# Earlier inputs in the load queues, and scores of a head pair on the two row halves of TensorE

## The chip, the cores and the metric

The kernel runs on one core of a Trainium2 chip. The metric is the device time of one execution in microseconds; several runs are taken and their median is given. One further execution is profiled: each instruction has its start, its length and what released it. A span is the time from the first to the last instruction of that execution.

The engines are TensorE (PE in the profile, its weight loads are PEld), VectorE (DVE), ScalarE (ACT), GpSimd (POOL) and SyncE (SP). Here SyncE does nothing but issue the loads of inputs and the stores; GpSimd issues the loads of weights beside its own work.

## The reference

Linear attention with a decay per head, in blocks, and behind it a layer norm with a two-layer MLP and a residual:

```
B, H, S, D = 4, 8, 768, 64                       # q, k, v in float32
for each block of the sequence:
    intra = ((q k^T) * Dmask) v                  # Dmask[i, j] = lam**(i-j) for i >= j, else 0
    inter = (q * lam**(i+1)) state
    out   = intra + inter
    state = lam**block * state + (k * lam**(block-1-i))^T v
x   = out as (B, S, H*D)                         # 512 wide
xn  = (x - mean) / sqrt(var + 1e-6) * g_ln
out = x + relu(xn @ w_ch1) @ w_ch2               # 512 -> 2048 -> 512
```

## The kernel before, in words

The 3072 rows (4 batches of 768) are cut into 24 tiles of 128 rows, six in a batch. Each tile passes five steps, and the heads go in four pairs, since two heads of 64 fill 128 partitions:

- `p0`/`bf_inputs` (lines 139 to 147, 289 to 292): GpSimd casts k to bf16 (`kb`), and multiplies q and v by powers of lam into bf16 (`qb`, `vb`). For tiles 4 and later `p0` also orders the load of tile t + 4.
- `p1` (149 to 168): PE transposes k and q, four transposes each. ScalarE copies k's transpose out of PSUM in two halves: head 0 of each pair to partitions 0 to 63 of one slot, head 1 to partitions 64 to 127 of another slot of `kTp`. The rest of `kTp` was set to zero once (lines 112 to 116), so that a matmul over all 128 partitions gives the score of one head alone.
- `p2` (170 to 196): the pair's k^T v (`pk`), from which VectorE and GpSimd make the next state (`Stmp`, `Sn`); eight score matmuls (line 192), four heads into each of two PSUM tiles `sc`; VectorE multiplies each by the mask into `mA`.
- `p3` (198 to 217): eight output matmuls on `mA` and `vb` (line 203), four on the state (207); ScalarE copies the result to `x`, VectorE makes mean and variance and the centred `xc`.
- `p4` (219 to 236): PE transposes `xc`, ScalarE copies it to `xT` of the tile's group and takes the root for the norm.

The MLP works on groups of tiles (`sizes`, line 284): `m1` (line 254) is layer 1 with ScalarE's relu behind it, `m2` (line 267) layer 2 of one tile in four parts of four matmuls, each part reading one of the four w2 chunks.

The order of the work is written out by hand (manual schedule; each engine works through its instructions in program order). Lines 309 to 354 place the first eight tiles and groups 0 to 3 one by one; `units` and `after` say which attention steps stand behind which MLP unit. From line 356 on a planner spreads the remaining attention steps (`round_of`: `p1`, `p3_p0`, `p2`, `p4`) evenly over the MLP units of groups 4 to 9, so that all steps of a group's tiles stand before its first `m1`.

Loads go through two queues. Inputs are issued by SyncE (k, q, v of a tile, 256 KB each, line 65), with six buffers each. Weights are issued by GpSimd (four chunks of w1, four of w2, lines 75 and 78), in its program order between casts. `load_tile(4, after_pool=True)` has GpSimd write one column of the buffer first, so SyncE's load waits until GpSimd has come that far. The steps concerned:

```python
run((p1, 0), (p2, 0), (p0, 2), (p1, 1), (p3, 0), (p2, 1))
load_w1(0); load_w1(1)
...
load_w1(3)
load_tile(4, after_pool=True)
for c in range(NWC): load_w2(c)
...
p0(4)            # casts of tile 4, behind three quarters of group 0's layer 1
```

Of the kernel before, what the change touches and what calls it, by code (L numbers as in the profile page):

```python
# [7 lines left out]
F32 = mybir.dt.float32  # L8
BF16 = mybir.dt.bfloat16
I32 = mybir.dt.int32  # L10
ALU = mybir.AluOpType
# [5 lines left out]
def kernel(  # L17
# [11 lines left out]
    nc = tc.nc  # L29
    B, H, S, D = q.shape  # L30
    C = 128
    nb = S // C
    NT = B * nb
    DM = H * D
    DF = moe_w_ch1.shape[1]
    NP = H // 2
# [9 lines left out]
    const = ctx.enter_context(tc.tile_pool(name="const", bufs=1))  # L46
    inp = ctx.enter_context(tc.tile_pool(name="inp", bufs=6))
    wk = ctx.enter_context(tc.tile_pool(name="wk", bufs=3))
    xp = ctx.enter_context(tc.tile_pool(name="xp", bufs=11))
    gp = ctx.enter_context(tc.tile_pool(name="gp", bufs=2))  # L50
    ps = ctx.enter_context(tc.tile_pool(name="ps", bufs=1, space=PSUM))


    qkv_in = {}

    def load_tile(t, after_pool=False):
        b, c = divmod(t, nb)
        got = {}
        for name, src in (("k", k), ("q", q), ("v", v)):
            f = inp.tile([128, H, D], F32, tag=name + "in", name=name + "in")  # L60
            if after_pool:

                nc.gpsimd.memset(f[:, 0, 0:1], 0.0)
                after_pool = False
            nc.sync.dma_start(f, src[b, :, c * C:(c + 1) * C, :].rearrange("h p d -> p h d"))
            got[name] = f
        qkv_in[t] = got
# [6 lines left out]
    def load_w1(c):  # L74
        nc.gpsimd.dma_start(w1[c], moe_w_ch1[:, c * W1C:(c + 1) * W1C].rearrange("(k p) f -> p k f", p=128))
# [20 lines left out]
    tril = const.tile([128, 128], F32)  # L96
# [12 lines left out]
    nc.vector.memset(eps_t, eps)  # L109
    lamC = const.tile([128, NP, 128], F32)  # L110
    nc.vector.memset(lamC, 0.0)
    kTp = []
    for i in range(2):
        kt = const.tile([128, NP, 2, 128], BF16, name=f"kTp{i}")
        nc.vector.memset(kt, 0.0)
        kTp.append(kt)

    lnlam = const.tile([128, H], F32)
    nc.scalar.activation(lnlam, lam_b, ACT.Ln)
# [4 lines left out]
    lam_c = const.tile([128, H], F32)  # L124
    nc.scalar.activation(lam_c, lnlam, ACT.Exp, scale=float(C))
    sqrt_first = const.tile([128, 1], F32)
    nc.scalar.activation(sqrt_first, eps_t, ACT.Sqrt)
    lam_cp = lam_c.rearrange("p (a two) -> p a two", two=2)
    nc.vector.tensor_copy(lamC[0:64, :, 0:64], lam_cp[0:64, :, 0:1].to_broadcast([64, NP, 64]))
    nc.vector.tensor_copy(lamC[64:128, :, 64:128], lam_cp[64:128, :, 1:2].to_broadcast([64, NP, 64]))  # L130


    st = {}
# [2 lines left out]
    mv_keep = {}  # L136
    xT_of = {}

    def bf_inputs(t):
        f = qkv_in.pop(t)  # L140
        kb = wk.tile([128, H, D], BF16, tag="kb", bufs=4, name="kb")
        nc.gpsimd.tensor_copy(kb, f["k"])  # L142
        qb = wk.tile([128, H, D], BF16, tag="qb", name="qb")
        nc.gpsimd.tensor_tensor(qb, f["q"], lam_q[:, :, None].to_broadcast([128, H, D]), op=ALU.mult)  # L144
        vb = wk.tile([128, H, D], BF16, tag="vb", bufs=4, name="vb")
        nc.gpsimd.tensor_tensor(vb, f["v"], lam_v[:, :, None].to_broadcast([128, H, D]), op=ALU.mult)  # L146
        st[t] = dict(qb=qb, kb=kb, vb=vb)

    def p1(t):
        s = st[t]  # L150
        tk = ps.tile([128, NP, 128], BF16, tag="aux", bufs=2, name="tk")
        for p in range(NP):
            nc.tensor.transpose(tk[:, p, :], s["kb"][:, 2 * p:2 * p + 2, :], ident)  # L153
        kT = kTp[t % 2]
        nc.scalar.copy(kT[0:64, :, 0, :], tk[0:64, :, :])  # L155
        nc.scalar.copy(kT[64:128, :, 1, :], tk[64:128, :, :])  # L156
        if t < 4:
            tq = ps.tile([128, NP, 128], BF16, tag="mm", bufs=3, name="tq")
        else:
            tq = ps.tile([128, NP, 128], BF16, tag="aux", bufs=2, name="tq")  # L160
        for p in range(NP):
            nc.tensor.transpose(tq[:, p, :], s["qb"][:, 2 * p:2 * p + 2, :], ident)  # L162
        qT = wk.tile([128, NP, 128], BF16, tag="qT", name="qT")
        if t < 4:
            nc.scalar.copy(qT, tq)
        else:
            nc.vector.tensor_copy(qT, tq)  # L167
        s["kT"], s["qT"] = kT, qT

    def p2(t):  # L170
        s = st[t]
        c = t % nb
        s["S"] = state.get("S") if c > 0 else None
        if c < nb - 1:
            pk = ps.tile([128, NP, 128], F32, tag="aux", bufs=2, name="pk")
            for p in range(NP):
                nc.tensor.matmul(pk[:, p, :], lhsT=s["kb"][:, 2 * p:2 * p + 2, :], rhs=s["vb"][:, 2 * p:2 * p + 2, :],  # L177
                                 start=(p == 0), stop=(p == NP - 1), skip_group_check=True)
            Sn = wk.tile([128, NP, 128], BF16, tag="S", name="Sn")
            if c == 0:  # L180
                nc.vector.tensor_tensor(Sn, pk, lamC, op=ALU.mult)
            else:
                tmp = wk.tile([128, NP, 128], F32, tag="Stmp", bufs=2, name="Stmp")
                nc.vector.tensor_tensor(tmp, pk, state["S"], op=ALU.add)  # L184
                nc.gpsimd.tensor_tensor(Sn, tmp, lamC, op=ALU.mult)  # L185
            state["S"] = Sn
        mA = wk.tile([128, H, 128], BF16, tag="mA", name="mA")
        for half in range(2):
            sc = ps.tile([128, H // 2, 128], F32, tag="sc", bufs=2, name="sc")
            for i in range(H // 2):  # L190
                h = half * (H // 2) + i
                nc.tensor.matmul(sc[:, i, :], lhsT=s["kT"][:, h // 2, h % 2, :], rhs=s["qT"][:, h // 2, :],  # L192
                                 start=(i == 0), stop=(i == H // 2 - 1), skip_group_check=True)
            nc.vector.tensor_tensor(mA[:, half * (H // 2):(half + 1) * (H // 2), :], sc,  # L194
                                    tril[:, None, :].to_broadcast([128, H // 2, 128]), op=ALU.mult)
        s["mA"] = mA

    def p3(t):
        s = st[t]
        po = ps.tile([128, H, D], F32, tag="po", bufs=1, name="po")  # L200
        inter = s["S"] is not None
        for h in range(H):
            nc.tensor.matmul(po[:, h, :], lhsT=s["mA"][:, h, :], rhs=s["vb"][:, h, :],  # L203
                             start=(h == 0), stop=(not inter and h == H - 1), skip_group_check=True)
        if inter:
            for p in range(NP):
                nc.tensor.matmul(po[:, 2 * p:2 * p + 2, :], lhsT=s["qT"][:, p, :], rhs=s["S"][:, p, :],  # L207
                                 start=False, stop=(p == NP - 1), skip_group_check=True)
        x = xp.tile([128, DM], F32, tag="x", name="x")
        nc.scalar.copy(x, po.rearrange("p h d -> p (h d)"))  # L210
        stats = wk.tile([128, 6], F32, tag="stats", name="stats")
        nc.vector.bn_stats(stats, x)  # L212
        mv = xp.tile([128, 2], F32, tag="mv", name="mv")
        nc.vector.bn_aggr(mv, stats)
        xc = wk.tile([128, DM], BF16, tag="xc", name="xc")
        nc.vector.scalar_tensor_tensor(xc, in0=x, scalar=mv[:, 0:1], in1=g_row, op0=ALU.subtract, op1=ALU.mult)  # L216
        s["xc"], s["mv"], s["x"] = xc, mv, x
# [63 lines left out]

        return m1, m2

    sizes = [2, 2, 1, 1, 2, 3, 3, 4, 4, 2]
    groups = [list(range(sum(sizes[:i]), sum(sizes[:i + 1]))) for i in range(len(sizes))]
    assert groups[-1][-1] == NT - 1
    group_of = {t: g for g, ts in enumerate(groups) for t in ts}

    def p0(t):
        if t > 3 and t + 4 < NT:  # L290
            load_tile(t + 4)
        bf_inputs(t)


    def p3_p0(t):
        p3(t)
        if t + 3 < NT:
            p0(t + 3)

    def round_of(j):  # L300
        steps = [(p1, j), (p3_p0, j - 1), (p2, j), (p4, j - 2)]
        return [(f, t) for f, t in steps if t < NT]

    def run(*steps):
        for f, *a in steps:
            f(*a)


    p0(0)
    p0(1)  # L310
    run((p1, 0), (p2, 0), (p0, 2), (p1, 1), (p3, 0), (p2, 1))
    load_w1(0)
    load_w1(1)
    run((p1, 2), (p3, 1))
    p0(3)
    load_w1(2)
    run((p2, 2), (p4, 0), (p1, 3), (p3, 2), (p2, 3), (p4, 1))
    load_w1(3)
    load_tile(4, after_pool=True)
    for c in range(NWC):  # L320
        load_w2(c)
    load_tile(5, after_pool=True)
# [5 lines left out]
    def m1s(f, c):  # L328
        for u in range(c * m1a.count // NWC, (c + 1) * m1a.count // NWC):
            f(u)  # L330
# [3 lines left out]
    m1s(m1a, 1)  # L334
    p4(3)
    m1s(m1a, 2)
    p0(4)
    for c in range(3):
        m1s(m1b, c)
    m1s(m1a, 3)  # L340
# [14 lines left out]

    steps = []
    for j in range(8, NT + 2):
        steps += [s for s in round_of(j) if s not in ((p3_p0, 7), (p4, 7), (p4, 6))]

    def upto(g):  # L360
        return steps.index((p4, groups[g][-1])) + 1 if g < len(groups) else len(steps)
# [47 lines left out]
```

## Time and profile before

| | us |
|---|---|
| median of 3 runs (lowest to highest) | 247.38 (247.32 to 247.84) |
| the profiled execution | 246.76 |
| its span | 245.0 |
| PE busy in it | 219.0 (89%) |
| ACT / DVE / POOL busy | 121.1 / 112.9 / 92.9 |

Busy shares are means over a start in which inputs arrive one by one, a stretch in which weights and inputs are loaded together, and a long stretch of matmuls. PE's granted clock has two levels here, 1.2 and 2.4 GHz; the view by stage gives their mean as a share of 2.4. The ends of matmuls are modelled, so starts are the surer numbers: in the chain of waits a group of matmuls runs to the start of the next, in the timeline to the modelled end of its last.

### The profile page before, as it was taken

Reading aid. Unit: us, or ns where it says so; the run is one execution under the profiler, and the core shown is the slowest. Engines: PE = TensorE matmul, PEld = TensorE weight load, DVE = VectorE, ACT = ScalarE, POOL = GpSimd, SP = SyncE. Lnnn points to the kernel's source line nnn. Section 1 sums busy time; section 2 is a strip of 40 time slices with the busy share of each in tenths; the row PEclk is TensorE's granted clock in tenths of the full one; section 3 lists DMA queues with packets and bytes.
Section 4 is the critical chain, followed back from the end, with each engine's and each line's share of the span. In section 5 each row is a group of like instructions: output and inputs, shape, how many; then the busy total and the mean of one; then the engine's idle time right before and its main releaser. Section 6 shows DMA issues by size and latency. Waiting matters only on the chain.

```text
span 245.0 us, 4603 instructions
## 1 busy us (share of the span) xinstructions
PE 219.0 (89%) x1856; PEld 142.2 (58%) x1856; DVE 112.9 (46%) x217; ACT 121.1 (49%) x236; POOL 92.9 (38%) x107
## 2 busy tenths in 40 slices
PE   0676894499999897999999999999999999999993
PEld 0565683354587586767755676555555544444851
DVE  3366700033547656798547655475346531122111
ACT  5745775002175366657863487427862247611520
POOL 2779710159500866791566293063322000000000
PEclk9999999689999999999999999999999999999999
DMA  6999999999899999329951960111001120012102
GB/s 127 236 195 146 147 188 196 218 210 210 188 300 208 235 229 219 67 63 237 221 84 43 225 120 4 43 47 43 0 3 43 43 86 3 0 43 88 43 0 86
DMA packets 83012, 29.91 MB, mean 122 GB/s; under 512 B 75568, under 2 KB 79920, under 8 KB 82992
## 3 DMA queue, kind: packets, MB, share of 16 engines
q1 hardware_dynamic: 78624, 25.43, 48.0%
q0 software_dynamic: 4224, 4.19, 10.7%
q8 instruction: 14, 0.23, 0.4%
q14 instruction: 6, 0.05, 0.1%
q10 hardware_dynamic: 144, 0.00, 0.0%
HBM read 27.53 MB, written 6.29 MB: 138 GB/s over the span
## 4 chain that ended last, share of the span: by engine, by line
PE 76%; DMA 8%; ACT 6%; DVE 5%; POOL 2%; issue 2%; DVEq 0%; SPq 0%; ACTq 0%
PE pm L267 33%; PE pm L254 28%; DMA qin<-in_q_dram 7%; PE sc L192 4%; PE po L203 2%; PE xt L230 2%; PE tk L153 2%; PE tq L162 2%; PE po L207 2%; PE pk L177 1%; DVE stats L212 1%; DMA lam_b<-in_lam_dram 1%; ACT kTp L155 1%; ACT x L210 1%; ACT kTp L156 1%
## 5 line engine op out<-in xcount | busy, mean ns | idle before, releaser
L254 PE MATMUL pm<-xT,w 128*128 128x256 bf16 (+3 forms) x640 | 92.6, 298 | 0.7 <-ACT xT L231 0.7
L267 PE MATMUL pm<-w,hT 128*128 128x512 bf16 x384 | 90.5, 381 | 0.0
L257 ACT ACTIVATE hT<-pm 128x512 bf16<-128x512 f32 (+1 forms) x104 | 58.1, 564 | 41.2 <-PE pm L254 40.6
L254 PEld LDWEIGHTS <-w 128*128 128x128 bf16 x640 | 56.9, 99 | 23.8 <-issue 0.8
L267 PEld LDWEIGHTS <-hT 128*128 128x128 bf16 x384 | 36.1, 98 | 36.1 <-issue 0.6
L185 POOL TENSOR_TENSOR Sn<-Stmp,lamC 128x512 bf16<-128x512 f32 x16 | 20.4, 1273 | 69.0 <-DVE Stmp L184 69.0
L212 DVE BATCH_NORM_STATS2 stats<-x 128x6 f32<-128x512 f32 x24 | 16.7, 695 | 46.2 <-ACT x L210 46.1
L278 DVE SCALAR_TENSOR_TENSOR o<-pm,rstd,x 128x512 f32<-128x512 f32 (+1 forms) x25 | 18.0, 725 | 32.7 <-PE pm L267 32.5
L231 ACT COPY xT<-xt 128x512 bf16<-128x512 bf16 x24 | 14.0, 584 | 37.1 <-PE xt L230 37.0
L194 DVE TENSOR_TENSOR mA<-sc,tril 128x512 bf16<-128x512 f32 x48 | 30.7, 680 | 0.0
L144 POOL TENSOR_TENSOR qb<-qin,lam_q 128x512 bf16<-128x512 f32 x24 | 25.8, 1074 | 12.1 <-DMA qin<-in_q_dram 8.6
L146 POOL TENSOR_TENSOR vb<-vin,lam_v 128x512 bf16<-128x512 f32 x24 | 25.5, 1060 | 3.4 <-DMA vin<-in_v_dram 3.0
L155 ACT COPY kTp<-tk 64x512 bf16<-64x512 bf16 x24 | 13.7, 572 | 16.9 <-PE tk L153 16.8
L210 ACT COPY x<-po 128x512 f32<-128x512 f32 x24 | 14.1, 586 | 14.7 <-PE po L207 11.0
L142 POOL CAST kb<-kin 128x512 bf16<-128x512 f32 x24 | 16.6, 690 | 10.8 <-DMA kin<-in_k_dram 10.7
L216 DVE SCALAR_TENSOR_TENSOR xc<-x,mv,g_row 128x512 bf16<-128x512 f32 x24 | 20.2, 840 | 0.9
L162 PE MATMUL tq<-ident,qb 128*128 128x128 bf16 x96 | 10.4, 237 | 11.1 <-POOL qb L144 9.5
L167 DVE COPY qT<-tq 128x512 bf16<-128x512 bf16 x20 | 8.4, 419 | 21.5 <-PE tq L162 21.5
L153 PE MATMUL tk<-ident,kb 128*128 128x128 bf16 x96 | 10.2, 234 | 7.6 <-POOL kb L142 7.6
L192 PE MATMUL sc<-qT,kTp 128*128 128x128 bf16 x192 | 16.4, 234 | 0.3 <-ACT kTp L156 0.2
L192 PEld LDWEIGHTS <-kTp 128*128 128x128 bf16 x192 | 13.5, 106 | 1.3 <-ACT kTp L156 0.4
L156 ACT COPY kTp<-tk 64x512 bf16<-64x512 bf16 x24 | 13.9, 580 | 0.6
(43 smaller groups left out, 127.0 us busy)
## 6 DMA issues: line engine op xcount, KB each, us to landing
kin<-in_k_dram SPq DMA_DIRECT2D x24, 256.0 KB, 4.8
qin<-in_q_dram SPq DMA_DIRECT2D x24, 256.0 KB, 5.1
vin<-in_v_dram SPq DMA_DIRECT2D x24, 256.0 KB, 5.1
out_dram<-o SPq DMA_DIRECT2D x23, 256.0 KB, 2.2
w<-in_moe_w_ch_dram POOLq DMA_DIRECT2D x8, 512.0 KB, 8.7
g_row<-in_moe_g_ln_dram SPq DMA_DIRECT2D x1, 256.0 KB, 4.8
out_dram<-o SPq DMA_DIRECT2D x2, 128.0 KB, 1.7
lam_b<-in_lam_dram ACTq DMA_DIRECT2D x1, 4.0 KB, 3.0
```

Source lines behind the costliest of these rows:

```text
L142: nc.gpsimd.tensor_copy(kb, f["k"])
L144: nc.gpsimd.tensor_tensor(qb, f["q"], lam_q[:, :, None].to_broadcast([128, H, D]), op=ALU.mult)
L146: nc.gpsimd.tensor_tensor(vb, f["v"], lam_v[:, :, None].to_broadcast([128, H, D]), op=ALU.mult)
L185: nc.gpsimd.tensor_tensor(Sn, tmp, lamC, op=ALU.mult)
L192: nc.tensor.matmul(sc[:, i, :], lhsT=s["kT"][:, h // 2, h % 2, :], rhs=s["qT"][:, h // 2, :], start=(i == 0), stop=(i == H // 2 - 1), skip ...
L194: nc.vector.tensor_tensor(mA[:, half * (H // 2):(half + 1) * (H // 2), :], sc, tril[:, None, :].to_broadcast([128, H // 2, 128]), op=ALU.mult)
L212: nc.vector.bn_stats(stats, x)
L216: nc.vector.scalar_tensor_tensor(xc, in0=x, scalar=mv[:, 0:1], in1=g_row, op0=ALU.subtract, op1=ALU.mult)
L254: nc.tensor.matmul(pm[:, b, :], lhsT=w1[n // W2K][:, kk, (n % W2K) * 128:(n % W2K + 1) * 128], rhs=xT_of[g][:, kk, 0:N], start=(b == 0 and ...
L257: nc.scalar.activation(hT[:, u * NB:(u + 1) * NB, 0:N], pm, ACT.Relu)
L267: nc.tensor.matmul(acc[i], lhsT=hT[:, kk, i * 128:(i + 1) * 128], rhs=w2[kk // W2K][:, kk % W2K, :], start=(kk == 0), stop=(kk == KB - 1))
L278: nc.vector.scalar_tensor_tensor(o[:, sl], in0=a[:, sl], scalar=rstd, in1=x[:, sl], op0=ALU.mult, op1=ALU.add)
```

## The change

- k is cast by VectorE for tiles 0 and 1 and by ScalarE for tiles 2 and 3; GpSimd casts k from tile 4 on, and q and v as before.
- The loads of w1 chunks and of tile 4 move: chunk 0 behind tile 2's casts, chunk 1 and then tile 4's inputs behind tile 3's, chunks 2 and 3 behind the next steps. `p0(4)` (GpSimd's casts of tile 4) moves ahead of the issues of w2. Tiles 5 to 7 are loaded behind w2, as before; tiles 8 and 9 are ordered together in `p0(5)`.
- k's transposes are kept compact: one copy of 128 partitions per tile into `kT`, no zeros. A score matmul takes the 64 partitions of its head, so the two heads of a pair use the upper and the lower row half of PE, one after the other in program order, each into its own PSUM tile. `mA` is laid out by even and odd heads.
- `sizes` becomes [2, 2, 1, 1, 2, 2, 3, 4, 4, 3], and in the planner `p4` comes one round earlier up to tile 10.

```diff
+    def in_k(t, eng):
+        kb = wk.tile([128, H, D], BF16, tag="kb", bufs=4, name="kb")
+        (eng.copy if eng is nc.scalar else eng.tensor_copy)(kb, qkv_in[t]["k"])
+        st[t] = dict(kb=kb)
+
+    def in_qv(t):
         f = qkv_in.pop(t)
-        kb = wk.tile([128, H, D], BF16, tag="kb", bufs=4, name="kb")
-        nc.gpsimd.tensor_copy(kb, f["k"])
...
-        kT = kTp[t % 2]
-        nc.scalar.copy(kT[0:64, :, 0, :], tk[0:64, :, :])
-        nc.scalar.copy(kT[64:128, :, 1, :], tk[64:128, :, :])
+        kT = wk.tile([128, NP, 128], BF16, tag="kT", name="kT")
+        nc.scalar.copy(kT, tk)
...
+        mA = wk.tile([128, 2, NP, 128], BF16, tag="mA", name="mA")
+        sc = [ps.tile([128, NP, 128], F32, tag="sc", bufs=2, name=f"sc{e}") for e in range(2)]
+        for p in range(NP):
+            for e in range(2):
+                half = slice(e * D, (e + 1) * D)
+                nc.tensor.matmul(sc[e][:, p, :], lhsT=s["kT"][half, p, :], rhs=s["qT"][half, p, :],
+                                 start=(p == 0), stop=(p == NP - 1), skip_group_check=True)
+        for e in range(2):
+            nc.vector.tensor_tensor(mA[:, e], sc[e], tril[:, None, :].to_broadcast([128, NP, 128]), op=ALU.mult)
...
-            nc.tensor.matmul(po[:, h, :], lhsT=s["mA"][:, h, :], rhs=s["vb"][:, h, :],
+            nc.tensor.matmul(po[:, h, :], lhsT=s["mA"][:, h % 2, h // 2, :], rhs=s["vb"][:, h, :],
...
-    sizes = [2, 2, 1, 1, 2, 3, 3, 4, 4, 2]
+    sizes = [2, 2, 1, 1, 2, 2, 3, 4, 4, 3]
...
-        if t > 3 and t + 4 < NT:
-            load_tile(t + 4)
-        bf_inputs(t)
+        for n in {4: (), 5: (8, 9)}.get(t, (t + 4,)):
+            if n < NT:
+                load_tile(n)
+        in_k(t, nc.gpsimd)
+        in_qv(t)
...
-        steps = [(p1, j), (p3_p0, j - 1), (p2, j), (p4, j - 2)]
+        steps = [(p1, j), (p3_p0, j - 1), (p2, j)]
+        if j <= 11:
+            steps.append((p4, j - 1))
+        elif j > 12:
+            steps.append((p4, j - 2))
...
+    run((p1, 0), (p2, 0), (p1, 1), (p3, 0))
+    in_k(2, nc.scalar)
+    in_qv(2)
     load_w1(0)
+    run((p2, 1), (p1, 2), (p3, 1))
+    in_k(3, nc.scalar)
+    in_qv(3)
     load_w1(1)
...
+    load_tile(4, after_pool=True)
+    run((p2, 2), (p4, 0), (p1, 3), (p3, 2))
     load_w1(2)
...
     load_w1(3)
-    load_tile(4, after_pool=True)
+    run((p2, 3), (p4, 1), (p0, 4))
     for c in range(NWC):
         load_w2(c)
     load_tile(5, after_pool=True)
...
     m1s(m1a, 2)
-    p0(4)
```

## Rows read from the trace of the kernel before

**Rows 1.** Work by stage: stretch, engines' busy us (instructions), granted clock, DMA share, GB/s.
```profile
40.00:46.60 6.60, 0.64 (x6) 0.58 (x7) 0.00 (x0) 1.02 (x2) 1.04 (x1) 0.84 1.21 196
46.60:60.00 13.40, 13.40 (x82) 7.47 (x81) 4.10 (x8) 2.56 (x5) 8.36 (x9) 0.82 1.09 215
75.00:100.00 25.00, 21.81 (x283) 18.34 (x282) 15.89 (x30) 14.33 (x27) 14.51 (x15) 1.00 1.09 222
150.00:175.00 25.00, 25.00 (x196) 14.18 (x195) 14.01 (x27) 13.42 (x28) 8.50 (x9) 1.00 0.09 32
```

**Rows 2.** The chain of waits in order of time: start us, us, what.
```profile
28.69 16.11 DMA qin<-in_q_dram
...
49.99 1.59 PE pm L267 x4
...
52.25 2.59 PE pm L267 x12
...
135.28 0.23 PE po L203 x8
...
137.69 0.45 PE sc L192 x8
```

**Rows 3.** Timeline of PE, 25 to 64 us: start, us, work [idle before <-releaser].
```profile
25.16 1.91 PE L254 MATMUL pm<-xT,w 128*128 128x256 bf16 x16 [0.67 <-ACT xT L231]
...
45.96 0.61 PE L162 MATMUL tq<-ident,qb 128*128 128x128 bf16 x4 [6.39 <-POOL qb L144]
...
46.37 3.62 PE L254 MATMUL pm<-xT,w 128*128 128x256 bf16 x16
...
63.99 0.39 PE L153 MATMUL tk<-ident,kb 128*128 128x128 bf16 x4
```

**Rows 4.** Timeline of GpSimd and of SyncE's queue, 15 to 32 us.
```profile
15.57 1.04 POOL L146 TENSOR_TENSOR vb<-vin,lam_v 128x512 bf16<-128x512 f32 x1
...
17.78 1.68 POOL L75 DMA_DIRECT2D w<-in_moe_w_ch_dram  x2
...
22.53 0.80 POOL L75 DMA_DIRECT2D w<-in_moe_w_ch_dram  x1
...
28.17 2.97 POOL L78 DMA_DIRECT2D w<-in_moe_w_ch_dram  x4
...
28.27 0.37 SPq L65 DMA_DIRECT2D kin<-in_k_dram  x1
```

**Rows 5.** Issue to landing: w1 chunks 0 and 1, chunk 2, w2's four, tile 4's k, q.
```profile
DMA to landing us min/median/max: 5.6/6.8/8.0
...
DMA to landing us min/median/max: 6.7/6.7/6.7
...
DMA to landing us min/median/max: 9.4/13.9/17.9
...
DMA to landing us min/median/max: 9.2/9.2/9.2
...
DMA to landing us min/median/max: 16.1/16.1/16.1
```

**Rows 6.** Timeline of PE, 78 to 96 us, where it waited.
```profile
78.53 0.38 PE L230 MATMUL xt<-ident,xc 128*128 128x128 bf16 x4 [0.47 <-DVE qT L167]
...
85.28 0.40 PE L230 MATMUL xt<-ident,xc 128*128 128x128 bf16 x4 [0.86 <-DVE xc L216]
...
88.79 0.22 PE L192 MATMUL sc<-qT,kTp 128*128 128x128 bf16 x1
89.23 0.56 PE L192 MATMUL sc<-qT,kTp 128*128 128x128 bf16 x7 [0.22 <-ACT kTp L156]
...
95.85 0.38 PE L162 MATMUL tq<-ident,qb 128*128 128x128 bf16 x4 [1.64 <-DVE Stmp L184]
```

**Rows 7.** Groups by line: work xcount | busy us, mean ns | idle before us, releaser.
```profile
L194 DVE TENSOR_TENSOR mA<-sc,tril 128x512 bf16<-128x512 f32 x48 | 30.7, 680 | 0.0
...
L156 ACT COPY kTp<-tk 64x512 bf16<-64x512 bf16 x24 | 13.9, 580 | 0.6
```

More of the change, by code (lines that the diff above doesn't have):

```diff
@@ L111 @@
     nc.vector.memset(lamC, 0.0)
[L112 to L116, printed above, removed]
     lnlam = const.tile([128, H], F32)
@@ L127 @@
     nc.scalar.activation(sqrt_first, eps_t, ACT.Sqrt)
-    lam_cp = lam_c.rearrange("p (a two) -> p a two", two=2)
-    nc.vector.tensor_copy(lamC[0:64, :, 0:64], lam_cp[0:64, :, 0:1].to_broadcast([64, NP, 64]))
-    nc.vector.tensor_copy(lamC[64:128, :, 64:128], lam_cp[64:128, :, 1:2].to_broadcast([64, NP, 64]))
     st = {}
@@ L137 @@
     xT_of = {}
-    def bf_inputs(t):
+    def in_k(t, eng):
[3 more added lines that the diff above has]
+    def in_qv(t):
         f = qkv_in.pop(t)
-        kb = wk.tile([128, H, D], BF16, tag="kb", bufs=4, name="kb")
-        nc.gpsimd.tensor_copy(kb, f["k"])
         qb = wk.tile([128, H, D], BF16, tag="qb", name="qb")
@@ L146, in bf_inputs @@
         nc.gpsimd.tensor_tensor(vb, f["v"], lam_v[:, :, None].to_broadcast([128, H, D]), op=ALU.mult)
-        st[t] = dict(qb=qb, kb=kb, vb=vb)
+        st[t].update(qb=qb, vb=vb)
     def p1(t):
@@ L186, in p2 @@
             state["S"] = Sn
[L187 to L195, printed above, removed]
+        mA = wk.tile([128, 2, NP, 128], BF16, tag="mA", name="mA")
[7 more added lines that the diff above has]
+            nc.vector.tensor_tensor(mA[:, e], sc[e], tril[:, None, :].to_broadcast([128, NP, 128]), op=ALU.mult)
         s["mA"] = mA
@@ L306, in run @@
             f(*a)
-    p0(0)
-    p0(1)
-    run((p1, 0), (p2, 0), (p0, 2), (p1, 1), (p3, 0), (p2, 1))
+    for t in range(2):
+        in_k(t, nc.vector)
+        in_qv(t)
+    lam_cp = lam_c.rearrange("p (a two) -> p a two", two=2)
+    nc.vector.tensor_copy(lamC[0:64, :, 0:64], lam_cp[0:64, :, 0:1].to_broadcast([64, NP, 64]))
+    nc.vector.tensor_copy(lamC[64:128, :, 64:128], lam_cp[64:128, :, 1:2].to_broadcast([64, NP, 64]))
+    run((p1, 0), (p2, 0), (p1, 1), (p3, 0))
+    in_k(2, nc.scalar)
+    in_qv(2)
     load_w1(0)
+    run((p2, 1), (p1, 2), (p3, 1))
+    in_k(3, nc.scalar)
+    in_qv(3)
     load_w1(1)
-    run((p1, 2), (p3, 1))
-    p0(3)
+    load_tile(4, after_pool=True)
+    run((p2, 2), (p4, 0), (p1, 3), (p3, 2))
     load_w1(2)
-    run((p2, 2), (p4, 0), (p1, 3), (p3, 2), (p2, 3), (p4, 1))
     load_w1(3)
-    load_tile(4, after_pool=True)
+    run((p2, 3), (p4, 1), (p0, 4))
     for c in range(NWC):
@@ L357 @@
     for j in range(8, NT + 2):
-        steps += [s for s in round_of(j) if s not in ((p3_p0, 7), (p4, 7), (p4, 6))]
+        steps += [s for s in round_of(j) if s not in ((p3_p0, 7), (p4, 7))]
     def upto(g):
```

## The prediction, on record before the result was known

> **What bounds the kernel now.** I read the busy time by stage first. From 150 to 175 us TensorE (PE) is busy for the whole 25.00 us at a granted clock of 1.00, while VectorE, ScalarE and GpSimd each stay under 15 and the DMA share is 0.09 [rows 1]. There the end moves only with PE's own work. Two earlier stretches differ: from 40.0 to 46.6 PE works 0.64 of 6.60 us with the DMA share at 1.21, and from 75 to 100 it works 21.81 of 25.00 [rows 1]. What follows the last matmul (one VectorE step and the last store) the change does not touch, and I leave it out.
>
> The chain of waits names the cause of the first hole: it runs for 16.11 us through one DMA, the q input of tile 4, issued at 28.69 [rows 2]. PE's timeline has the other side: tile 4's q transposes start at 45.96 after 6.39 us of waiting for GpSimd's `qb` [rows 3]. Behind the hole the granted clock falls, 0.84 and then 0.82 on average [rows 1], that is, to the 1.2 GHz level for some of the time. Sixteen layer-1 matmuls take 3.62 us there and 1.91 at the higher level [rows 3]; four layer-2 matmuls take 1.59 where a third of 2.59, 0.86, is normal [rows 2]. So the hole costs 6.39 + 1.71 + 0.73 = 8.8 us, and no more than that is to be had from it.
>
> Why is that input late? Tile 4's k is issued at 28.27, just when GpSimd issues the four layer-2 weight chunks (28.17 to 31.14) [rows 4]. They share the DMA engines: k lands 9.2 us and q 16.1 us after its issue, so at 37.5 and 44.8, 7.3 us apart, while the weight chunks land at 37.6 (28.17 + 9.4) to 48.3 (30.4 + 17.9), one in 3.6 us [rows 5]. With inputs alone in the queues, 215 GB/s [rows 1], a 256 KB third of a tile needs 1.2 us.
>
> **The change, part by part.** (a) *Order of loads.* GpSimd now casts no k for tiles 0 to 3 (VectorE and ScalarE do) and issues w1 chunk 0 behind tile 2's `vb`, which ends at 15.57 + 1.04 = 16.6 in place of 17.78 [rows 4]. Then come the issue (0.8), one state update (1.2, the time that it took between `vb`'s end and the issue at 17.78), and tile 3's two casts (2 x 1.04): chunk 1 is issued at 20.7. In before it went out with chunk 0, so this chunk is some 2 us later. Tile 4's inputs follow at 21.7 in place of 28.27; chunks 2 and 3 at about 23 and 24, behind one more state update (chunk 2 went out at 22.53 [rows 4]).
>
> Landing: a chunk by itself needs 5.6 us from issue, and chunks 0 and 2 land at 23.4 and 29.2, so 2.9 us each [rows 4, 5]. Chunk 1: 20.7 + 5.6 = 26.3; then beside tile 4, 3.6 each: 29.9 and 33.5. PE starts layer 1 at 25.16 [rows 3] and wants chunk 1 some 2.5 us later, chunk 2 at 30.5, chunk 3 only after three more group passes: waits of 0 to 0.5 us, which come out of slack in front of w2 and which I cost at nothing. Tile 4: k at 21.7 + 9.2 = 30.9; q has 2.6 of its 7.3 us beside the weights until 33.5, and the other 64% alone takes 0.8: 34.3; v at 35.5.
>
> Now the added wait. w2's issues stand on GpSimd behind tile 4's casts, which wait for tile 4's k, q and v. Queued behind them are the four w2 issues, the release of tile 5's load, and the state update of tile 4; PE's layer 2 waits for the first, tile 5 for the second. `vb` ends at 36.6, w2 chunk 0 lands 5.6 later at 42.2, chunk 1 at 45.1, chunks 2 and 3 beside tile 5 at 48.7 and 52.3. PE, without the hole, reaches the end of layer 1 at 39.6 (45.96 - 6.39) + 0.4 (tile 4's transposes) + 1.8 = 41.8. Its layer-2 parts (three units of 0.86 each) then run 42.2 to 44.8, with tile 4's attention steps (0.45 and 0.23 [rows 2] and two steps of four 128-column matmuls, 0.22 each as half of the eight: 1.1) to 45.9, 45.9 to 48.7, 48.7 to 51.3, and 52.3 to 54.9: less than 2 us of waiting in pieces of at most 1.0, so I expect the clock to stay up. Two more units (1.7) bring it to tile 5's transposes at 56.6; before they start at 63.99 [rows 3]. Gain **7.4 us**. Bounds: 8.8 above (the whole hole), and below as w2 is late, 2 if each step is 1.3 us longer. Tile 5 is late next: its last third lands at about 54, its `vb` ends at 55, within 1.6 us of being needed.
>
> (b) *Scores on two row halves.* Eight score matmuls take 0.45 us of the chain per tile; the eight output matmuls behind them, with as many weight loads but half the columns, take 0.23 [rows 2]. If the two heads of a pair run side by side, eight take what the weight loads allow, 0.23, and the 20 tiles inside the PE-bound part (4 to 23) give back 20 x 0.22 = 4.4. If they run one behind the other, nothing. If PE must empty itself on going to half rows and back, a lone matmul's 0.22 in the trace against 0.056 in the row of eight [rows 6, 2] bounds that at 0.16 twice per tile: 0.33 - 0.22 = 0.11 lost, 2.2 us over 20 tiles. The nearest row is the output matmuls', which says loads do not stand in the way; I keep two thirds, **3.0 us**, for some cost at the switch.
>
> The Trainium skill speaks on both sides. "TensorE: Matmul & The Clock Gate" (Part 3, Packing small matmuls) has matmuls on different row groups start about 4 ns apart, and by that alone the sum would be the 4.4. "TensorEngine Tiling (Array Packing)" (Key Properties) says that changing the tiling mode drains TensorE, and this kernel changes it twice a tile; no row here shows a switch. By the second rule the sum is that of the third rival.
>
> (c) *k transposes in one copy.* ScalarE makes one 128-partition copy in place of two of 0.58 us [rows 7]: 0.58 less per tile on an engine that is not the bound. It counts where PE waited: of 3.2 us idle from 75 to 100, the 0.47 at 78.53 (the transposes had to wait for a buffer) goes in part, and the 0.22 at 89.23 goes [rows 6].
>
> (d) *New order and sizes of groups.* The first three-tile group becomes two, the last two becomes three; the count of matmul columns is the same, so 0. Tile 10's transposes no longer stand directly behind tile 9's state matmuls, where `tq` waited 1.64 for `Stmp` [rows 6]: gone. Against it, tiles 8 to 10 transpose their normalised x one round sooner, with about 2.2 us between their output matmuls and that; at 85.28 such a step waited 0.86 [rows 6]. And the even and odd heads now lie in different halves of `mA`, so the output matmuls need both mask products (0.68 each [rows 7]) from the start, where half the heads could begin after one. Idle of 3.2 becomes about 2.2: gain **1.0**, bounds -1 and +2.
>
> **Sum.** The profiled execution took 246.76 us (span 245.0 and 1.7 around it): 246.76 - 7.4 - 3.0 - 1.0 = 235.4. The median of the runs, 247.38, lies 0.6 above that execution; the forecast is **236.0**.
>
> **Rivals** (times on the runs' scale).
> 1. *Pairs side by side without a price.* 4.4 in place of 3.0, and the hole gone to within half a microsecond: 233.5. For it: the 0.23 row. Against: w2's late issue.
> 2. *Pairs one behind the other.* 0 in place of 3.0: 239.0. For it: no row shows two matmuls at once.
> 3. *The switch drains PE.* 2.2 lost in place of 3.0 gained: 241.2. It would show as weight loads standing still before each tile's first score and first output matmul.
> 4. *Layer-2 weights become the hole* (the slower side). If weights hold tile 4's inputs back to the end (9.2 + 7.3 + 7.3 us after 21.7: 45.5), w2 starts 10 us later than I have it. Each microsecond that tile 4's v lands after 35.5 costs one. PE then idles from 41.8 to 52, the clock falls as it did (2.4 at 1.71 + 0.73), and tile 5 starts at 66.6: 246.76 + 2.6 + 2.4 - 4.0 + 0.6 = 248.4. It decides from a landing at about 44.4. For it: q's 7.3 us. Against: only three weight chunks are then in the queues, where before there were five.
> 5. *The hole shrinks little* (w2 lands 3 to 5 us later than worked out, no fall of the clock): 239 to 241 with (b) as forecast, up to 244 without.
>
> **How the numbers follow.** Chances: forecast 0.42 (its own range 234.5 to 238), rival 1 0.18, rival 2 0.14, rival 3 0.09, rival 5 0.09, rival 4 0.08. Runs of this kernel tell 0.2% (0.5 us) from no change. Rival 4 is slower in most of its spread, 0.07, with 0.02 within 0.2%; all others are faster: 0.91. The range from 232.5 to 241.5 takes in the full 8.8 and 4.4 on one side, and rivals 2 and 3 on the other; what is outside is rival 4 and the worse half of rival 5.
>
> **What would show it.** Tile 5's k transposes at 56 to 58; no wait of PE over 2 us between 25 and 60, the granted clock at 1.00 throughout; w2 chunks issued near 37 and tile 4's v landing near 35.5. Eight score matmuls in 0.25 to 0.35 us of the chain (0.45 says rival 2; idle or still weight loads around them say rival 3). PE's idle time from tile 5's transposes to 95 at about 2 us. The prediction is wrong if w2's first chunk lands after 46, or if PE in its bound part gains nothing per tile.

## The result, and the profile after

The changed kernel takes 239.12 us in the median of four runs (238.12 to 240.05), the kernel before 247.35 beside it: a ratio of 0.967, 95% interval 0.9622 to 0.9718. The forecast of 236.0 was 3.1 us too fast; the measured time lies inside the stated range of 232.5 to 241.5. The profiled execution took 239.36 us (span 237.6), 7.4 less than the one before; the forecast's own sum was 11.4 less.

Work by stage, the first three stretches of [rows 1] (stretch, busy us of PE, PEld, DVE, ACT, POOL with instructions, granted clock, DMA share, GB/s):

```profile
40.00:46.60 6.60, 6.60 (x66) 5.14 (x65) 1.26 (x3) 3.85 (x7) 0.06 (x1) 1.00 1.17 183
46.60:60.00 13.40, 13.40 (x82) 6.48 (x80) 5.52 (x10) 1.95 (x4) 6.69 (x8) 1.00 1.11 209
75.00:100.00 25.00, 24.11 (x248) 16.44 (x246) 14.81 (x29) 11.90 (x23) 18.28 (x21) 1.00 1.09 228
```

The hole of [rows 1, 3] is gone: PE is busy from 40 to 60 us at a granted clock of 1.00. The timeline of PE answers to [rows 3], with the same four steps and those around them. First comes the row of the kernel before for the 80 layer-1 matmuls, then the changed kernel:

```profile
30.45 8.90 PE L254 MATMUL pm<-xT,w 128*128 128x256 bf16 x80
```

```profile
25.21 0.60 PE L225 MATMUL xt<-ident,xc 128*128 128x128 bf16 x4
26.49 2.99 PE L249 MATMUL pm<-xT,w 128*128 128x256 bf16 x16 [0.67 <-ACT xT L226]
...
29.78 0.39 PE L225 MATMUL xt<-ident,xc 128*128 128x128 bf16 x4
30.00 1.91 PE L249 MATMUL pm<-xT,w 128*128 128x256 bf16 x16
33.24 0.40 PE L225 MATMUL xt<-ident,xc 128*128 128x128 bf16 x4 [1.33 <-DVE xc L211]
33.48 8.90 PE L249 MATMUL pm<-xT,w 128*128 128x256 bf16 x80
...
42.44 0.39 PE L156 MATMUL tq<-ident,qb 128*128 128x128 bf16 x4
42.66 1.91 PE L249 MATMUL pm<-xT,w 128*128 128x256 bf16 x16
44.41 1.03 PE L262 MATMUL pm<-w,hT 128*128 128x512 bf16 x4
...
57.83 0.39 PE L148 MATMUL tk<-ident,kb 128*128 128x128 bf16 x4
```

Tile 5's k transposes start at 57.83; before it was 63.99 [rows 3], so 6.2 us were won in front. But layer 1 starts at 26.49, 1.3 us later than before, and its first block takes 2.99 us, since PE was still at the lower level: four transposes take 0.60 at 25.21 and 0.39 at 29.78. (The view by stage prints 1.00 for this stretch. In this trace the records of the granted clock begin only at 28.76 us, with its first change, so in the start the durations have to be read.) With the wait of 1.33 for tile 3's `xc`, the 80 matmuls that began at 30.45 before begin at 33.48, 3.0 later. From there to tile 5's transposes it is 63.99 - 30.45 = 33.5 us before and 57.83 - 33.48 = 24.4 after: 9.2 less. No wait for w2 is left: PE reaches layer 2 at 44.41, and w2's first chunk lands at 36.2 + 6.4 = 42.6.

GpSimd, which answers to [rows 4], VectorE beside it, and SyncE's queue; then issue to landing (min, median, max) for w1's and for w2's four chunks [rows 5]:

```profile
18.88 1.05 POOL L139 TENSOR_TENSOR qb<-qin,lam_q 128x512 bf16<-128x512 f32 x1
19.88 1.04 POOL L141 TENSOR_TENSOR vb<-vin,lam_v 128x512 bf16<-128x512 f32 x1
20.86 0.81 POOL L75 DMA_DIRECT2D w<-in_moe_w_ch_dram  x1
...
35.19 1.04 POOL L141 TENSOR_TENSOR vb<-vin,lam_v 128x512 bf16<-128x512 f32 x1 [2.55 <-DMA vin<-in_v_dram]
```

```profile
18.93 2.54 DVE L211 SCALAR_TENSOR_TENSOR xc<-x,mv,g_row 128x512 bf16<-128x512 f32 x1
```

```profile
21.81 0.37 SPq L65 DMA_DIRECT2D kin<-in_k_dram  x1
```

```profile
DMA to landing us min/median/max: 5.5/6.8/10.5
```

```profile
DMA to landing us min/median/max: 6.4/9.7/14.0
```

The loads went as worked out: chunk 1 at 20.86 (20.7), tile 4 at 21.81 (21.7). Tile 1's `xc` on VectorE takes 2.54 us, while GpSimd makes `qb` and `vb` without a pause; tile 2's takes 0.75. Tile 3's takes 1.61: it starts at 31.58, and GpSimd's `qb` of tile 4 at 31.60.

### The profile page after: what moved, and what is told of

Its sections match the earlier page's. It is cut to its first block, busy times and chain, and to the rows that moved or that the text cites. A ratio compares the mean times of both kernels' runs of the same rounds, so it can differ in the third digit from the quotient of the medians.

```text
span 237.6 us, 4583 instructions
## 1 busy us (share of the span) xinstructions
PE 216.4 (91%) x1856; PEld 134.2 (56%) x1856; DVE 114.2 (48%) x217; ACT 110.1 (46%) x214; POOL 90.0 (38%) x103
## 4 chain that ended last, share of the span: by engine, by line
PE 83%; DVE 6%; SPq 3%; DMA 2%; ACT 2%; issue 2%; POOL 0%; DVEq 0%
PE pm L262 34%; PE pm L249 33%; PE sc L187 3%; SPq L65 3%; PE xt L225 3%; DMA qin<-in_q_dram 2%; PE po L198 2%; DVE xc L211 2%; PE tq L156 2%; PE po L202 2%; DVE stats L207 2%; PE tk L148 2%; PE pk L171 2%; ACT x L205 1%; DVE mA L190 1%
## 5 line engine op out<-in xcount | busy, mean ns | idle before, releaser
L252 ACT ACTIVATE hT<-pm 128x512 bf16<-128x512 f32 (+1 forms) x104 | 58.7, 565 | 37.2 <-PE pm L249 36.4
L249 PEld LDWEIGHTS <-w 128*128 128x128 bf16 x640 | 56.1, 99 | 25.0 <-issue 0.8
L262 PEld LDWEIGHTS <-hT 128*128 128x128 bf16 x384 | 35.4, 98 | 36.0
L211 DVE SCALAR_TENSOR_TENSOR xc<-x,mv,g_row 128x512 bf16<-128x512 f32 x24 | 21.5, 894 | 0.9
L150 ACT COPY kT<-tk 128x512 bf16<-128x512 bf16 x24 | 14.0, 582 | 14.3 <-PE tk L148 14.2
L133 POOL CAST kb<-kin 128x512 bf16<-128x512 f32 x20 | 12.7, 633 | 4.3 <-DMA kin<-in_k_dram 4.1
L198 PEld LDWEIGHTS <-mA 128*128 128x128 bf16 x192 | 9.3, 102 | 7.0 <-DVE mA L190 3.3
L198 PE MATMUL po<-vb,mA 128*128 128x64 bf16 x192 | 10.8, 199 | 2.5 <-DVE mA L190 2.5
L148 PEld LDWEIGHTS <-kb 128*128 128x128 bf16 x96 | 7.6, 104 | 9.8 <-DVE kb L133 5.5
```

Source lines behind the costliest of these rows:

```text
L198: nc.tensor.matmul(po[:, h, :], lhsT=s["mA"][:, h % 2, h // 2, :], rhs=s["vb"][:, h, :], start=(h == 0), stop=(not inter and h == H - 1), ...
L249: nc.tensor.matmul(pm[:, b, :], lhsT=w1[n // W2K][:, kk, (n % W2K) * 128:(n % W2K + 1) * 128], rhs=xT_of[g][:, kk, 0:N], start=(b == 0 and ...
L252: nc.scalar.activation(hT[:, u * NB:(u + 1) * NB, 0:N], pm, ACT.Relu)
L262: nc.tensor.matmul(acc[i], lhsT=hT[:, kk, i * 128:(i + 1) * 128], rhs=w2[kk // W2K][:, kk % W2K, :], start=(kk == 0), stop=(kk == KB - 1))
```

## The experiments

All times are medians, each beside runs of the kernel before on the same chip (246.0 to 246.8). As the measure, the changed kernel again:

> The changed kernel again, as the measure for the others of this chip. Both theories: 239.1 us, 0.967 of before.

Measured 239.34 (ratio 0.9705, 0.9678 to 0.9731).

### Scores over all rows again

```diff
-        kT = wk.tile([128, NP, 128], BF16, tag="kT", name="kT")
-        nc.scalar.copy(kT, tk)
+        kT = kTp[t % 2]                        # zeroed once
+        nc.scalar.copy(kT[0:64, :, 0, :], tk[0:64, :, :])
+        nc.scalar.copy(kT[64:128, :, 1, :], tk[64:128, :, :])
...
-  lhsT=s["kT"][half, p, :], rhs=s["qT"][half, p, :]
+  lhsT=s["kT"][:, p, e, :], rhs=s["qT"][:, p, :]
```

> The changed kernel, but each score matmul takes all 128 rows of a zero-padded k transpose, as before the change (two copies by ScalarE again); order, PSUM tiles and mask layout stay. Theory A (TensorE pays about 0.096 us on going to half rows and 0.092 on coming back, which eats what the pairs save): eight scores go from 0.33 back to 0.45 us of the chain, but the matmul ahead and the one behind lose their extra 0.19; net 0.008 us a tile, so 239.1 to 239.5, no difference from the changed kernel. Rival B (switching is free, each tile gained the 0.12 us that the chain shows, and the gain that is missing went elsewhere): 20 x 0.12 = 2.4 us slower, 241.5.

Measured 240.36 (0.9744, 0.9711 to 0.9777), some 1 us above the changed kernel, with intervals that overlap: between the two theories. The profiles part it. From tile 5's transposes to the end of the span it is 238.7 - 57.45 = 181.2 us here and 238.0 - 58.20 = 179.8 in the measure. The waits of PE from 58 us to the last matmuls (total, times, longest), first here, then in the changed kernel:

```profile
PE xt L230 <- DVE xc L216: 1.4, 2, 0.9
PE xt L230 <- DVE qT L167: 1.0, 2, 0.5
PE tq L162 <- DVE Sn L181: 0.4, 1, 0.4
PE sc L192 <- ACT kTp L156: 0.2, 1, 0.2
```

```profile
PE xt L225 <- DVE xc L211: 1.6, 3, 0.9
PE tq L156 <- DVE Sn L175: 0.4, 1, 0.4
```

3.0 against 2.0. (The second fence is from the first profile of the changed kernel. The measure's own profile has the same two lines, and 0.5 us at three places that the view gives to no releaser; there the record of one matmul is missing.) So of the 1.4 us about 1.0 is waits: 1.0 for a buffer that VectorE's `qT` copy frees and 0.2 for the second k copy, less 0.2 for `xc`. They come with the edit; that the second copy brings them, and not the full rows, is argued from what is waited for, since no run has half rows with two copies. Little is left for PE's own work. The starts say the same for one tile with state update, at the same place of the plan: all rows (this run), then half rows (the changed kernel):

```profile
124.89 0.39 PE L177 MATMUL pk<-vb,kb 128*128 128x128 bf16 x4
125.11 0.61 PE L192 MATMUL sc<-qT,kTp 128*128 128x128 bf16 x8
125.56 0.81 PE L254 MATMUL pm<-xT,w 128*128 128x384 bf16 x4
126.21 0.39 PE L230 MATMUL xt<-ident,xc 128*128 128x128 bf16 x4
```

```profile
123.94 0.39 PE L171 MATMUL pk<-vb,kb 128*128 128x128 bf16 x4
124.26 0.40 PE L187 MATMUL sc<-qT,kT 64*128 64x128 bf16 x8
124.59 0.82 PE L249 MATMUL pm<-xT,w 128*128 128x384 bf16 x4
125.25 0.39 PE L225 MATMUL xt<-ident,xc 128*128 128x128 bf16 x4
```

From the first score to the next MLP matmul it is 0.45 with all rows and 0.33 with half rows; the gain of 0.12 is real. But the four state matmuls ahead take 0.22 and 0.32. In all 0.67 and 0.65, and the MLP matmuls behind take 0.01 longer to the next group's start: from `pk` to `xt` it is 1.32 and 1.31. That leaves 0.01 a tile, some 0.2 us over 20 tiles. (The kernel before has the same 0.22 and 0.45, at 128.60 and 128.82.) The group of scores alone shows a gain that the groups around it pay.

### The same scores in another order

```diff
-        for p in range(NP):
-            for e in range(2):
+        for e in range(2):
+            for p in range(NP):
```

> The changed kernel with the same eight half-row score matmuls in another order: the four heads on the lower rows first, then the four on the upper, so neighbours use the same half. Theory A (a pair runs side by side only when neighbours use different halves): start to start 56 ns in place of 28, 8 x 0.028 x 20 tiles = 4.5 us slower, 243.6. Rival C (a half-row matmul takes 28 ns whatever stands beside it): 239.1.

Measured 239.88 (0.9725, 0.9692 to 0.9758): no difference that can be told. My theory A was wrong in this point: it wanted 243.6. The row of this kernel:

```profile
124.27 0.41 PE L187 MATMUL sc<-qT,kT 64*128 64x128 bf16 x8
124.61 0.82 PE L249 MATMUL pm<-xT,w 128*128 128x384 bf16 x4
```

0.34 for the eight, as when they alternate. So it is not the neighbour in program order that makes the overlap. Rival C's time came true as well, but not its reason. In this trace the signals with which the lower four and the upper four matmuls report their end come 0.06 us apart (124.68 and 124.74, and likewise in the other tiles); one group behind the other, at 28 ns a matmul, they would be 0.11 apart. The eight start in pairs, 0.06 us from pair to pair. So the two halves ran side by side although four of the one stand ahead of four of the other in the program.

### More changes of mode

```diff
+        for p in range(NP):
+            for e in range(2): matmul(sc[e][:, p, :], ...)     # half rows
+            if c < nb - 1: matmul(pk[:, p, :], ...)            # all rows
```

> The changed kernel with the same matmuls, but the four full-row k^T v matmuls of a tile stand one behind each pair of scores, so a tile with a state update goes to half rows four times and back four times, not once. Theory A: 6 more changes of mode of 0.094 us on the 16 such tiles from tile 4 on = 9.0 us slower, 248. Rival B (switching is free): 239.1 to 239.5.

Measured 251.07 (1.0185, 1.015 to 1.0219), 11.7 us above the measure, more than the 9.0 of theory A; rival B is out. One tile:

```profile
131.31 0.23 PE L174 MATMUL sc<-qT,kT 64*128 64x128 bf16 x2
131.47 0.23 PE L177 MATMUL pk<-vb,kb 128*128 128x128 bf16 x1
131.63 0.23 PE L174 MATMUL sc<-qT,kT 64*128 64x128 bf16 x2
...
132.44 0.23 PE L177 MATMUL pk<-vb,kb 128*128 128x128 bf16 x1
132.51 0.81 PE L250 MATMUL pm<-xT,w 128*128 128x384 bf16 x4
```

From the first pair to the MLP 1.20 us; the same matmuls in two runs take 0.33 + 0.22 = 0.55. The 0.65 between are six more changes of mode, **0.11 us each**. Two of them per tile, 0.22, are as much as the overlap saves (eight at 0.056, the spacing with all rows, take 0.45; four pairs take half of that).

### The score part alone

```diff
 # kernel before, loads, order and groups unchanged
+ half-row scores, one copy of kT, mA by even and odd heads
```

> The kernel before with the half-row scores, the compact k transposes and the even/odd mask layout alone; loads, order and groups as before. Theory A (mode changes eat the overlap): 20 x 0.008 = 0.2 us, and up to 0.7 from ScalarE's shorter copies between 75 and 100 us: 246.5 to 247.4. The prediction's term (3.0): 244.4.

Measured 245.2 against 246.78 (0.9938, 0.9915 to 0.996): more than theory A's 0.2 to 0.9, half of the 3.0 predicted. In the profile tile 5's k transposes stay at 64.01, and 1.1 us are won after them (243.9 - 64.01 = 179.9 against 181.0), in PE's waits: `tq` for the buffer 0.7 in place of 1.6, the copies' 0.5 and 0.2 gone, against 0.4 of new waits for `mA` and 0.2 more for `xc`. The two profiled executions, 246.76 and 245.58, differ by 1.2; the half microsecond by which the medians differ more lies in no row of theirs. So the score part brings more than theory A gave it, and what it brings is in the waits.

### The late start of layer 1

```diff
+    load_w1(1)
     in_qv(3)
-    load_w1(1)
```

> The changed kernel with w1 chunk 1 issued by GpSimd ahead of tile 3's q and v casts, not behind them. In the changed kernel tile 1's xc took 2.54 us on VectorE where 0.75 is its usual length, while GpSimd made two casts without a pause. Theory D (VectorE's xc stands still while GpSimd's two-input casts run, which starts layer 1 late): in the 0.8 us of issuing xc runs through, 0.8 to 1.0 us; layer 1 starts near 24.9 in place of 26.49, and the end comes 1 to 2.5 us earlier, 236.6 to 238.1, less if w2 then binds. Rival E (xc's length has another cause): xc still 2 to 2.5 us, 239.1.

Measured 237.77 (0.9638, 0.9614 to 0.9663), 1.6 us under the measure, with intervals that do not overlap: theory D holds, E is out. VectorE and GpSimd in this run:

```profile
18.65 0.99 DVE L211 SCALAR_TENSOR_TENSOR xc<-x,mv,g_row 128x512 bf16<-128x512 f32 x1
```

```profile
18.66 0.80 POOL L75 DMA_DIRECT2D w<-in_moe_w_ch_dram  x1
19.48 1.06 POOL L139 TENSOR_TENSOR qb<-qin,lam_q 128x512 bf16<-128x512 f32 x1
```

`xc` is 0.99 in place of 2.54, and layer 1 starts at 23.94 in place of 26.49. The Trainium skill, "SBUF — State Buffer" (Who interferes with whom), has the rule: a VectorE operation with two inputs from SBUF contends with a GpSimd operation that reads SBUF for one port pair, which is locked by one of them at a time. The traces agree, and add that `xc` does not get its turn between two GpSimd operations that follow each other directly. It came 0.05 us behind `qb` and also stood behind the `vb` that followed: it ended at 21.47, 0.55 after `vb`. In the measure's profile it even started 0.16 ahead of `qb`, while GpSimd still made the next state (`Sn`), and took 2.76.

Against the measure, layer 1 starts 2.8 us sooner here (26.78 there), but tile 5's transposes only 1.2 us sooner (57.01 against 58.20): the first layer-1 block takes 3.57 us at the lower level, and PE waits 0.45 for a w2 chunk. So it is not the late `xc` alone that holds the level low. The run with the score part alone, with loads and order as before the change, has the same:

```profile
25.14 3.57 PE L248 MATMUL pm<-xT,w 128*128 128x256 bf16 x16 [0.67 <-ACT xT L225]
```

Two further steps on top of it: tile 3's x transposes behind the next layer-1 block, then w2 chunk 0 between tile 4's casts.

```diff
-    p4(3)
     m1s(m1a, 2)
+    p4(3)
```

> As with w1 chunk 1 early, and in addition tile 3's x transposes stand behind layer-1 block 2 of group 0 and not ahead of it, so that PE does not wait for tile 3's xc (1.33 us in the changed kernel). Theory D: that wait goes, 1 us faster than with w1 early alone, as far as the landing of w2 (42.6 to 52.5 us) allows: 236.0 to 237.5. Rival F (w2 binds): the same as w1 early alone, with waits of PE for w2's chunks.

```diff
+    in_qv(4, between=lambda: load_w2(0))
-    for c in range(NWC):
+    for c in range(1, NWC):
```

> As before it, and w2 chunk 0 is issued between tile 4's q and v casts, which fills the 3 us in which the queues run empty. If w2 binds (F): chunks land 3 us earlier and the end comes 1 to 2 us earlier than with the x transposes moved alone, 235 to 236.5. If it does not: no difference.

Measured 238.07 (0.963 to 0.9674) and 238.66 (0.9644 to 0.9691): no gain from either. In the first, PE's wait for tile 3's `xc` turned into one of 0.94 us for the copy of its transposes, and none for w2 is in its profile, so neither theory D nor F fits. In the second the first layer-1 block, begun at 24.64, takes 3.57 us, because PE is still at the lower level. So the next step was to give PE work in its gaps.

### Work in the gaps of the start

```diff
+    def warm(n):                         # result read by nobody
+        w = ps.tile([128, 512], F32, tag="mm", bufs=3, name="warm")
+        for i in range(n): nc.tensor.matmul(w, lhsT=ident, rhs=kb_of_tile_0, ...)
...
+        if t in (1, 2, 3): warm(t)       # in p1, behind the k transposes
...
-    run((p2, 1), (p1, 2), (p3, 1))
+    run((p2, 1), (warm, 2), (p1, 2), (p3, 1))
...
+    warm(1)
     m1s(m1a, 0)
```

> The kernel with w1 chunk 1, tile 3's x transposes and w2 chunk 0 moved, and in addition nine 512-column matmuls on data already there, whose result nobody reads, in the gaps of PE between 12 and 25 us (0.43 us each at the lower clock). Theory G (what keeps the moved loads from paying is the clock, which there came up only at 30.2 us, so that the first layer-1 block took 3.57 us in place of 1.91): the clock comes up before 25 us, the first block takes 1.9 to 2.2, tile 5's transposes start near 55 in place of 57.1, 236 to 237 us, and the runs spread less. Rival H (the clock is not moved by such work, or the w2 landings bind): clock up at 28 to 30, 238.0 to 238.9.

> The changed kernel with the same nine matmuls and nothing else moved. Theory G: the clock is up before layer 1 starts at 26.5, its first block takes 1.9 in place of 3.0 us, 1.0 to 1.5 us faster: 237.7 to 238.2. Rival H: 239.1 or more, since the added 3.9 us of work stand partly in the way.

Measured 237.73 (0.9656, 0.9629 to 0.9684) with the moved loads, and 239.0 (0.9683, 0.9651 to 0.9716) on the changed kernel. The first shows the mechanism of theory G, but not its 236 to 237, and its interval overlaps that of the kernel without the nine matmuls (0.9644 to 0.9691):

```profile
23.64 1.91 PE L263 MATMUL pm<-xT,w 128*128 128x256 bf16 x16 [0.46 <-ACT xT L240]
...
30.52 1.92 PE L263 MATMUL pm<-xT,w 128*128 128x256 bf16 x16 [1.66 <-DMA w<-in_moe_w_ch_dram]
```

The first block takes 1.91 us, at the higher level, and then PE waits 1.66 for w1 chunk 2: the loads bind next. In the second, layer 1 starts at 26.57 as before, and its time lies between the two theories. Theory G's mechanism failed there. PE reached the higher level early (tile 3's q transposes take 0.40 at 20.06), but then waited 2.35 us for `mA`, and the level fell. The view by stage for 22.4 to 29 us, and the first block:

```profile
22.40:29.00 6.60, 5.58 (x41) 3.90 (x42) 4.52 (x10) 1.89 (x4) 4.18 (x5) 0.50 1.15 194
```

```profile
26.57 3.15 PE L261 MATMUL pm<-xT,w 128*128 128x256 bf16 x16 [0.25 <-ACT xT L238]
```

### w1 chunk 2 ahead of tile 4's inputs

```diff
     in_qv(3)
+    load_w1(2)
     load_tile(4, after_pool=True)
...
-    load_w1(2)
     load_w1(3)
...
-    m1s(m1a, 2)
+    m1a(4)
     p4(3)
+    m1a(5)
```

> The kernel with moved loads and the nine extra matmuls, in which PE now waited 1.66 us for w1 chunk 2 and 0.94 for the copy of tile 3's x transposes. Here w1 chunk 2 is issued ahead of tile 4's inputs, and the x transposes stand in the middle of layer-1 block 2. Theory I (the landing of w1 chunk 2 binds): both waits go, tile 5's transposes start near 54 in place of 56.2, 235.2 to 236.2 us. Rival J (the queues are full from 20 us on, so what lands sooner makes tile 4's inputs or w2 later by as much): the wait turns up at w2 or at tile 4, 237 to 238.

Measured **236.88** (0.9609, 0.9581 to 0.9638), lowest of all, 2.5 us under the changed kernel's 239.34. Its interval touches that of the early-chunk run (0.9614 to 0.9663), so that the steps after that one pay together is likely, not shown. Both theories have a part: the wait for w1 is gone, but PE now waits at w2, and tile 5's transposes start at 55.5, not 54.

```profile
44.10 1.02 PE L276 MATMUL pm<-w,hT 128*128 128x512 bf16 x4 [0.25 <-DMA w<-in_moe_w_ch_dram]
...
48.13 0.81 PE L276 MATMUL pm<-w,hT 128*128 128x512 bf16 x3 [0.82 <-DMA w<-in_moe_w_ch_dram]
```

## Why the prediction was right, and where its sizes were off

- **(a), the order of loads, 7.4 predicted, 6.2 measured.** Right in its mechanism: the input wait and the low clock behind it went, 9.2 us from the 80 layer-1 matmuls on (the 8.8 of the prediction, and 0.4 of slower transposes and matmul ends beside them), and the issues came within 0.2 us of the times worked out. What took 3.0 us of it back was not w2's landing, as I had it, but the start: layer 1 began 1.3 us late (`xc` held up by GpSimd's casts), its first block ran in part at the lower level (1.1), and tile 3's `xc` was late (the rest). In the measure's profile the loss is 3.4 us and split otherwise: 1.6 late, 1.7 for a block of 3.57, and a wait of only 0.27 for tile 3's `xc`. I costed the moved casts by GpSimd's time alone and not by what VectorE does beside them. The early-chunk run shows the first of the three. Why the level is low at 26 us stays open: the early-chunk run and the score part alone have it without the late `xc`. So tile 5 came at 57.83, inside the 56 to 58 of the prediction, but by luck: a loss that it did not have stands where it had put the wait for w2.
- **(b), scores on row halves, 3.0 predicted, about 0.2 measured** in PE's own work. This term was mis-sized. Rival 3's mechanism is there: a change of mode costs 0.11 us, where the bound was 0.16. It does not lose the 2.2 of rival 3 but makes nothing, so the size is rival 2's; that the measured 239.1 stands on rival 2's 239.0 is chance, since the pairs do run side by side. I had kept two thirds of the gain because the output matmuls' row shows that weight loads are no limit; that row says nothing of the switch. The sign that I had named, eight scores in 0.25 to 0.35 us, came true (0.33) and misled, since the price stands in the groups around. By the prediction's last sign, no gain per tile in the bound part, this part of it was all but wrong (0.01 a tile). The Trainium skill's rule ("TensorEngine Tiling (Array Packing)", Key Properties: a change of mode drains TensorE) was the one to go by; the trace agrees as far as the price of a change goes.
- **(c) and (d), 1.0 predicted, about 1.0 measured** (181.0 - 179.8 = 1.2 us from tile 5 to the end, less 0.2 of (b)). The full-row run and the score part alone point to the single copy of `kT` as what brings it; as both edits change the rows too, that is argued. The new order of steps takes away the 1.64 of [rows 6] and puts new waits for `xc` in its place: with the old copies the waits are 3.0 us, as against 3.2 before. So (d) is about nothing, and the sum of the two came true with its parts otherwise than I had them.
- Rival 4 did not come: tile 4's v was there by 35.2 (its `vb` starts at 35.19), the 35.5 of the prediction.

The sum: 246.76 - 6.2 - 0.2 - 1.0 = 239.4, the profiled 239.36.

## What to carry to other kernels

Packing half-row matmuls pays only if a run of them is long against two changes of mode; at 0.11 us each, eight 128-column matmuls on 64 rows just break even. Look at the instructions ahead of the packed group too, for half of the price stands there. When casts are moved onto an engine's idle time, ask which operation of another engine they hold up; and when a load order is improved, the next limit (here PE's start at its lower clock, then the next weight chunk) takes back much of what is won, so move one load and read the trace again.

## What was unexpected of the hardware

- A change between all rows and half rows costs TensorE 0.10 to 0.11 us, on the way in as on the way out: in the run with more changes each group starts 0.16 us behind the last, where 0.056 is usual for one full-row matmul.
- The order of half-row matmuls in the program did not matter (0.33 and 0.34 us for eight); the two row halves ran side by side even with four of one half ahead of four of the other.
- A VectorE operation with two SBUF inputs that starts 0.05 us behind a GpSimd cast stood still for that cast and the next: 2.54 us in place of 0.75.
